# Attention and a mixture of experts on one core: an output's addition moved behind a search's comparisons, and the last expert's routing moved forward

## The chip, the cores and the metric

The kernel runs on one core of one Trainium2 chip. The metric is the device time of one execution in microseconds (us). Three executions of the kernel before took 903.22, 905.01 and 906.87 us, so the median is 905.01 us. One further execution was profiled; it took 904.79 us, of which the profile's span, from the first to the last instruction, is 903.0 us.

## What is computed

First an attention over 8 batches, 12 heads, 448 positions and a head size of 64, with scores squeezed by a tanh; then a mixture of 8 experts over the 3584 rows of 768 numbers that come out of it.

```
scores = cap * tanh((scale * q @ k.T) / cap)
attn   = exp(scores - max) / sum
x      = (attn @ v) as N x D                  # 3584 x 768
logits = x @ w_gate                           # 3584 x 8
order  = argsort(-logits.flatten())
for idx in order:                             # greedy, best pair first
    tok, e = idx // E, idx % E
    if assigned[tok] >= 0 or counts[e] >= cap: continue
    assigned[tok] = e; counts[e] += 1         # cap = 3584 / 8 = 448
for e in range(E):
    h = relu(x[assigned == e] @ w1[e])        # 448 x 1024
    out[assigned == e] = h @ w2[e]            # 448 x 768
```

The greedy assignment is sequential in the reference. The kernel does it expert by expert: it finds which expert fills up first, fixes that expert's 448 rows, takes them out, and goes on. So the experts come out in an order that the data sets, one every round, and each one's rows are known only when its search is done.

## The kernel before

The first 330 us or so are the attention and the gate's logits. From then on TensorE (PE) computes one expert after the other. The text calls the p-th expert in the order of routing "turn p", with p from 0 to 7.

**The two GEMMs of a turn.** A turn has 320 large matmuls, and a counter `now` counts them; `rt.place` is this counter modulo 320, "the place". `ffn1` has 8 units `f` of 18 matmuls (L855, 128 x 448), 144 in all: 6 chunks of the 768 inputs, times three products, because each fp32 operand is split in a high and a low part (`xgh`, `xgl` and `w1h`, `w1l`). `ffn2` has 8 units `u` (L883, 128 x 384): the token blocks 0 to 3 for the left half of the outputs (`hf` 0, `u` 0 to 3), then the same for the right half. Blocks 0 to 2 have 24 matmuls, block 3 (64 tokens) has 16. Its result is in two halves of 64 rows, so ScalarE (ACT) copies the lower one to `y` (L892) and VectorE (DVE) adds it to the upper one, which is still in PSUM (L893). The result tiles `psH` are three, in rotation; a unit's slot is free again when its last reader is done.

**The search beside it.** The routing of turn p+1 is computed while PE works on turn p. It is a generator (`phases0`): each `yield n` says after how many further matmuls the next piece is to be issued, a negative number gives an absolute place. A piece's instructions are put into the engines' queues in just that order, and each engine runs its own queue strictly in order. `select` is one search by thresholds, in rounds: DVE compares all values with 3 or 7 thresholds (L504, `cmpD`; ACT takes two of seven in later rounds, `cmpA`, L501), PE adds the counts up (L508), DVE picks the next thresholds (L512, L516). There are three searches for an expert, A, B and C; A has 4 rounds with 3, 7, 7 and 3 comparisons, and in its first two rounds DVE does all of them. A runs beside the second GEMM of a turn; B begins at its end, and its first L508 stands three matmuls into the next turn. `finalise` makes the list of rows out of the search's result: a few small DVE operations (L605 to L611), two matmuls (L617, L618), more DVE operations (L621 to L635), four matmuls (L639), and so on to `idx` (L651). The table `LK` holds the place at which `finalise` is issued, for each turn.

**The DMA turn of x.** As soon as a turn's rows are known, GpSimd (POOL) gathers them (`gather`, L790). PE needs x with the inputs on the partitions. From turn 3 on (`FT=3`) DMAs do that: four `planes` on ACT split the 32-bit numbers in 16-bit halves (L812, `pl`) and store them (L813, `xz`), and two transposed loads on the queue of SyncE (SP) bring them back (L816): the first after two planes, the second after four. `cutt` then makes `xgh` on ACT (L822) and `xgl` on DVE (L823), in unit `u` 6. The planes are issued 26, 34, 42 and 50 matmuls after the gather; they stand in the list `xq`, which `tick` looks through after each matmul: the entry at its head is run when the counter has reached its number.

**Weights.** SP loads `w1r` and `w2r` in pieces, four and three buffers of them; ACT makes the high part and POOL the low part of each (`cut`, L758 and L762, `w1l` and `w2l`). POOL also issues the scatter of finished outputs (L868).

The lines that the change touches are the table `LK` (L327), the `yield` in `finalise` (L614) and the addition in `ffn2` (L893).

Of the kernel before, what the change touches and what calls it, by code (L numbers as in the profile page):

```python
# [323 lines left out]


YL=[]
LK=(0,0,145,132,132,132,132,128); FT=3  # L327
ACF=1
LF=1
TA=0  # L330
# [2 lines left out]
class Routing:  # L333
# [267 lines left out]
    def finalise(s,wp,L,update):  # L601
        nc=s.nc; T=s.T; NC=s.NC; v=nc.vector
# [8 lines left out]
        v.tensor_scalar(ei,s.e8s[0:1],-1.0,8.0,op0=ALU.mult,op1=ALU.add)  # L611
        s.ei=ei
        if s.cur>=FT: s.early(s.cur,ei)
        yield 8 if s.cur==1 else 18 if s.cur>=FT else 12  # L614
        ps=s.psum()
        warm=(lambda n: s.warm(n)) if s.cur==0 else (lambda n: None)
        nc.tensor.matmul(ps[:112,0:2],s.lo,sc[:,:,NC-1],start=True,stop=False)  # L617
# [19 lines left out]
        ps=s.psum()  # L637
# [8 lines left out]
        ps=s.psum()  # L646
# [25 lines left out]
    def phases0(s,wp,L,turned):  # L672
        HA=[7,10]; HB=3
        for p in range(s.E):
# [5 lines left out]
            yield from (s.search(wp,turned if p==0 else ()) if p<s.E-1 else s.last(wp))  # L680
            yield -((p-1)*320+LK[p]) if p>1 else 4
            yield from s.finalise(wp,L,p<s.E-1)
# [3 lines left out]
def ffn_all(nc, tc, ctx, rt, xs, xz, w1, w2, out, ident, E, wp, deferred, xctx, gen):  # L686
# [44 lines left out]
    def need(p):  # L731
        while len(res)<=p: step()
# [67 lines left out]
    def xtr(p,c):  # L800
        if p>=E or c is None: return
        newx(p)
        gather(p)
        ps=pt.tile([128,512],F32,name="psX")
        for j,(o,n) in enumerate(TS):
            nc.tensor.transpose(ps[:,o:o+128],row(j)[:,c*128:c*128+128],ident)
        cutx(p,c,ps)
# [22 lines left out]
    def tick(n=1):  # L830
        cnt[0]+=n; bc[0]+=n; now[0]+=n
        if bc[0]>=BG:
            if pend: bc[0]=0; scatter(*pend.pop(0))
        if len(res)>cur[0]+1 and cur[0]+1 not in xgs:
            bc[0]=0; n=cur[0]+1; gather(n)
            if n>=FT:
                xq.extend((now[0]+TD+TJ*j,lambda j=j: planes(j)) for j in range(4))
        while xq and xq[0][0]<=now[0]: xq.pop(0)[1]()
        if cnt[0]>=hint[0]:
            cnt[0]=0; step()  # L840
# [23 lines left out]
    ons={}; scat=[]  # L864
# [9 lines left out]
    def ffn2(p,t,hf,cs,work={}):  # L874
        if p not in ons: ons[p]=(f2.tile([128,3*DM],F32,name="on"),f2.tile([64,DM],F32,name="on3"))
        ps=ph.tile([128,512],F32,name="psH")
        h=hh[p]
        o,n=TS[t]
        terms=((o,0),(512+o,0),(o,1)) if t<3 else ((o,0),(o,1))
        m=0; nm=FC*len(terms)  # L880
        for f in range(FC):
            for a,w in terms:
                nc.tensor.matmul(ps[:,:HD],h[:,f,a:a+128],spl[p,2,hf,f//2][w][:,f%2,:],start=(m==0),stop=(m==nm-1))  # L883
                m+=1
                tick()
                if m%8==4 and m//8<len(cs): xtr(p+1,cs[m//8])
                for z in work.get(m,()): z()
        cols=slice(hf*HD,hf*HD+HD)
        if t<3: nc.scalar.activation(ons[p][0][:,t*DM+hf*HD:t*DM+hf*HD+HD],ps[:,:HD],AF.Copy)  # L889
        else:  # L890
            y=f2.tile([64,HD],F32,name="y3",bufs=2)
            nc.scalar.activation(y,ps[64:128,:HD],AF.Copy)  # L892
            nc.vector.tensor_tensor(ons[p][1][:,cols],ps[:64,:HD],y,op=ALU.add)  # L893
    need(0)
    WG=3; NW=23; WJ=4
    for i in range(WG): load1(0,i)
# [13 lines left out]
    for p in range(E):  # L910
# [12 lines left out]
        if lastp:  # L923
            while pend: scatter(*pend.pop(0))
            ih=f2.tile([128,2],I32,name="ih")
            for k in range(2): nc.gpsimd.tensor_scalar(ih[:,k:k+1],res[p][0][:,2:3],2.0,float(k),op0=ALU.mult,op1=ALU.add)
            nc.gpsimd.drain()
            lp[0]=False
            out2=out.rearrange("n (q d) -> (n q) d",q=2)
            for t,hf in [(t,hf) for t in (3,0,1,2) for hf in range(2)]:  # L930
                ffn2(p,t,hf,[])
                if t==2: put(out2,ih[:,hf:hf+1],ons[p][0][:,t*DM+hf*HD:t*DM+hf*HD+HD])
                elif hf==1: scatter(p,t)
            break
        for u in range(8):
            if p+1<FT:
                if u==4: load1(p+1,0); load1(p+1,1)
                if u==5: load1(p+1,2); load2(p+1,0)
            if u==6:
                if p+1>=FT: load1(p+1,2); load2(p+1,0)  # L940
                load1(p+1,3)
            if u==7: load2(p+1,1)
            wk=({5:{14:[lambda: split1(p+1,0)]},6:{8:[lambda: split1(p+1,1)]}} if p+1<FT else {5:{2:[lambda: split1(p+1,0)],12:[lambda: split1(p+1,1)]}}).get(u,{})
            if p<1 and u==7: wk={15:[lambda: xtr(1,3)]}
            if p+1>=FT and not lastp:
                for m,k,c in {6:[(5,0,0),(9,1,0),(12,0,3),(15,1,3)]}.get(u,()): wk[m]=wk.get(m,[])+[lambda k=k,c=c: cutt(p+1,k,c,c+3)]
            ffn2(p,u%4,u//4,(CL if p<1 else CP)[u] if p+1<FT else [],wk)
            if u>3: pend.append((p,u%4))
# [59 lines left out]
```

## Time and profile before

| | |
|---|---|
| median of three executions | 905.01 us |
| profiled execution | 904.79 us |
| its span | 903.0 us |
| first L855 of turns 2 to 7 | 514.30, 581.58, 649.02, 714.74, 776.41, 838.28 us |
| granted TensorE clock over the span | 0.994 |

A row of a timeline gives the start in us, the duration, the engine, the line in the code, the operation, the tile written and the tiles read with their shapes, and in brackets how long the engine had stood idle before and what ended that. A row of waits gives the total, the number of times and the longest. Neighbouring matmuls overlap in the rows (0.34 us each, one every 0.17 us), so a wait is read from the starts.

### The profile page before, as it was taken

The numbers are of one execution on the slowest core, as the hardware profiler recorded it, in microseconds if no ns is written. First come the engines' busy times: TensorE is split into PE (matmuls) and PEld (weight loads), VectorE is DVE, ScalarE is ACT, GpSimd is POOL, SyncE is SP. The second block draws the span as 40 slices with busy tenths as digits, with TensorE's granted clock in tenths as the row PEclk, the third lists the DMA queues.
The fourth block names the chain that finished last, engine by engine and source line by source line (L and its number), as shares of the span: only waits on it lengthen the run. The fifth ranks groups of instructions, "written<-read, shape, count | busy, mean of one in ns | idle before, by whom it ended". The sixth has DMA issues, their size and how long they took to land.

```text
span 903.0 us, 17418 instructions
## 1 busy us (share of the span) xinstructions
PE 867.1 (96%) x6222; PEld 635.0 (70%) x6222; DVE 608.5 (67%) x2012; ACT 585.2 (65%) x836; POOL 350.6 (39%) x506
## 2 busy tenths in 40 slices
PE   7999999999999997899999999899899899999997
PEld 3333444444333345789989989889889889989997
DVE  3788888989888888766776776776776775240210
ACT  6998898989899948273582673573573664434521
POOL 7100000000000009482593492492492592774751
PEclk9999999999999999999999999999999999999999
DMA  8799999996994017751825525925925926927801
GB/s 120 116 133 136 133 172 171 140 171 118 201 170 70 1 61 244 246 160 52 277 75 171 163 71 158 293 75 157 287 82 166 296 63 179 310 71 202 287 10 53
DMA packets 321463, 136.84 MB, mean 152 GB/s; under 512 B 252288, under 2 KB 303232, under 8 KB 320864
## 3 DMA queue, kind: packets, MB, share of 16 engines
q1 hardware_dynamic: 312304, 106.59, 53.9%
q0 software_dynamic: 4656, 22.02, 7.2%
q10 hardware_dynamic: 4416, 7.11, 2.4%
q8 instruction: 49, 0.80, 0.4%
q14 instruction: 38, 0.31, 0.1%
HBM read 97.15 MB, written 31.65 MB: 143 GB/s over the span
## 4 chain that ended last, share of the span: by engine, by line
PE 76%; DVE 6%; issue 5%; DMA 5%; ACT 3%; SPq 3%; POOL 2%; ACTq 0%; POOLq 0%; DVEq 0%
PE psH L855 23%; PE psH L883 19%; PE psA L189 12%; PE psS L148 11%; PE psM L206 4%; DMA xg<-xs,idx 2%; PE psS L153 2%; DVE cmpD L504 2%; SPq L92 2%; ACT pl L812 1%; PE psM L37 1%; DMA w1r<-in_moe_w_dram 1%; DVE es L165 1%; DMA k<-in_k_dram 1%; PE psL L37 1%
## 5 line engine op out<-in xcount | busy, mean ns | idle before, releaser
L883 PE MATMUL psH<-w2h,hh 128*128 128x384 f32 x896 | 244.9, 343 | 0.0
L883 PE MATMUL psH<-w2l,hh 128*128 128x384 f32 x512 | 175.5, 343 | 0.0
L154 ACT ACTIVATE e<-psS 128x896 f32<-128x896 f32 x168 | 147.5, 909 | 30.5 <-PE psS L148 17.8
L883 PEld LDWEIGHTS psH<-w2h,hh 128*128 128x128 f32 x896 | 164.1, 191 | 0.2
L159 ACT ACTIVATE e<-e,bias 128x1792 f32<-128x1792 f32 (+2 forms) x74 | 147.2, 1991 | 2.0
L855 PE MATMUL psH<-xgh,w1h 128*128 128x448 f32 x384 | 143.4, 374 | 0.3 <-ACT xgh L827 0.3
L855 PE MATMUL psH<-xgh,w1l 128*128 128x448 f32 x384 | 141.5, 368 | 0.0
L855 PE MATMUL psH<-xgl,w1h 128*128 128x448 f32 x384 | 141.0, 367 | 0.0
L148 PE MATMUL psS<-tq,tk 64*64 64x448 f32 x1152 | 131.0, 549 | 6.1 <-ACT e L154 3.9
L762 POOL TENSOR_TENSOR w1l<-w1r,w1h 128x768 fp32r<-128x768 f32 x62 | 114.6, 1851 | 18.3 <-ACT w1h L758 13.0
L189 PE MATMUL psA<-e,nv 64*64 64x448 f32 x1104 | 120.3, 539 | 1.0 <-DVE xT L199 1.0
L762 POOL TENSOR_TENSOR w2l<-w2r,w2h 128x768 fp32r<-128x768 f32 x64 | 118.3, 1849 | 6.2 <-ACT w2h L758 6.0
L460 POOL TENSOR_SCALAR r_Bt<-r_b 112x4 f16<-112x4 int32 x1 | 0.2, 201 | 303.7 <-DVE rin L243 303.7
L165 DVE TENSOR_TENSOR es<-es,e 64x896 f32<-64x896 f32 (+2 forms) x74 | 100.3, 1356 | 2.6 <-ACT e L159 1.3
L883 PEld LDWEIGHTS psH<-w2l,hh 128*128 128x128 f32 x512 | 97.4, 190 | 0.0
L148 PEld LDWEIGHTS psS<-tq,tk 64*64 64x64 f32 x1152 | 43.6, 133 | 72.7 <-issue 38.0
L889 ACT ACTIVATE on<-psH 128x384 f32<-128x384 f32 x48 | 23.5, 490 | 104.1 <-PE psH L883 102.4
L863 DVE SCALAR_TENSOR_TENSOR hh<-psH,hh 128x64 fp32r<-128x64 f32 (+1 forms) x128 | 44.0, 385 | 65.3 <-ACT hh L861 63.4
L189 PEld LDWEIGHTS psA<-e,nv 64*64 64x64 f32 x1104 | 46.0, 133 | 59.5 <-issue 50.5
L868 POOL DMA_INDIRECT out_dram<-on,idx x31 | 32.5, 1047 | 123.1 <-ACT on L889 94.3
L855 PEld LDWEIGHTS psH<-xgh,w1h 128*128 128x128 f32 x384 | 72.6, 189 | 5.5 <-ACT xgh L827 0.5
L855 PEld LDWEIGHTS psH<-xgh,w1l 128*128 128x128 f32 x384 | 72.3, 188 | 5.6 <-POOL gap L760 0.2
(337 smaller groups left out, 1320.8 us busy)
## 6 DMA issues: line engine op xcount, KB each, us to landing
w1r<-in_moe_w_dram SPq DMA_DIRECT2D x64, 384.0 KB, 5.3
w2r<-in_moe_w_dram SPq DMA_DIRECT2D x32, 768.0 KB, 7.4
k<-in_k_dram SPq DMA_DIRECT2D x92, 112.0 KB, 3.4
q<-in_q_dram SPq DMA_DIRECT2D x92, 112.0 KB, 4.0
nv<-in_v_dram SPq DMA_DIRECT2D x72, 128.0 KB, 3.8
xz<-pl ACTq DMA_DIRECT2D x15, 384.0 KB, 3.2
xs<-xn SPq DMA_DIRECT2D x4, 1344.0 KB, 7.2
xs<-xn SPq DMA_DIRECT2D x4, 896.0 KB, 5.1
```

The source lines that it names most:

```text
L148: for c in range(2): nc.tensor.matmul(ps[c*64:c*64+64,h,:S],tks[g,0][hp,o,u*128+c*64:u*128+c*64+64],tks[g,1][hp,o,:],start=True,stop=True)
L154: nc.scalar.activation(ev(g,r),ps[:,:,:S],AF.Tanh,scale=sr[0])
L159: act=lambda: nc.scalar.activation(e,e,AF.Exp,scale=sr[1],bias=bias)
L165: t=es_t[g]; add=lambda o,a,b: nc.vector.tensor_tensor(o,a,b,op=ALU.add)
L189: nc.tensor.matmul(avp[g,o][h*64:h*64+64,:S],lhs,rhs[hp,h,:],start=(j==0 and x==0),stop=j==3)
L206: nc.tensor.matmul(ps[g*32:g*32+32,:S],lhs,rhs,start=first,stop=last)
L762: (eng or nc.gpsimd).tensor_tensor(view(l),r,view(h).bitcast(F32),op=ALU.subtract)
L855: nc.tensor.matmul(ps[:,:C],a[:,c,:],b[:,c,:],start=(m==0),stop=(m==DC*3-1)); m+=1
L863: nc.vector.scalar_tensor_tensor(h[:,d:d+b-a],ps[:,a:b],0.0,h[:,a:b].bitcast(F32),op0=ALU.max,op1=ALU.subtract)
L868: st=nc.gpsimd.indirect_dma_start(out=dst,out_offset=bass.IndirectOffsetOnAxis(ap=ix,axis=0),in_=src,in_offset=None)
L883: nc.tensor.matmul(ps[:,:HD],h[:,f,a:a+128],spl[p,2,hf,f//2][w][:,f%2,:],start=(m==0),stop=(m==nm-1))
L889: if t<3: nc.scalar.activation(ons[p][0][:,t*DM+hf*HD:t*DM+hf*HD+HD],ps[:,:HD],AF.Copy)
```

## The change

Three lines are changed.

```diff
-LK=(0,0,145,132,132,132,132,128); FT=3
+LK=(0,0,145,132,132,132,132,100); FT=3
...
         if s.cur>=FT: s.early(s.cur,ei)
-        yield 8 if s.cur==1 else 18 if s.cur>=FT else 12
+        yield 8 if s.cur==1 else 30 if s.cur==7 else 18 if s.cur>=FT else 12
...
             y=f2.tile([64,HD],F32,name="y3",bufs=2)
             nc.scalar.activation(y,ps[64:128,:HD],AF.Copy)
-            nc.vector.tensor_tensor(ons[p][1][:,cols],ps[:64,:HD],y,op=ALU.add)
+            add=lambda: nc.vector.tensor_tensor(ons[p][1][:,cols],ps[:64,:HD],y,op=ALU.add)
+            if hf==0 and FT-1<=p<E-1: xq.append((now[0]+20,add))
+            else: add()
```

The addition of `u` 3 (`hf` 0, place 232) is put into `xq` for 20 matmuls later, in turns 2 to 6. On DVE, in turn 2, beside search A's first and second round:

```order
 L512 SCALAR_TENSOR_TENSOR fl,th<-psR,r_H8A 128x4
 L516 TENSOR_SCALAR r_H8A,nt<-r_C8A,th 128x7
-L893 TENSOR_TENSOR on_6498<-psH,y_6697 64x384
 L504 TENSOR_SCALAR cmpD,r_ce_309<-r_VAt,th 128x224
 L504 TENSOR_SCALAR cmpD,r_ce_309<-r_VAt,r_H8A 128x224 x6
 L512 SCALAR_TENSOR_TENSOR fl,th<-psR,r_H8A 128x8
 L516 TENSOR_SCALAR r_H8A,nt<-r_C8A,th 128x7
+L893 TENSOR_TENSOR on_6498<-psH,y_6697 64x384
 L504 TENSOR_SCALAR cmpD,r_ce_310<-r_VAt,th 128x224
 L504 TENSOR_SCALAR cmpD,r_ce_310<-r_VAt,r_H8A 128x224 x4
```

The addition stood ahead of the second round's seven comparisons; now it stands behind them and behind that round's result, ahead of the third round's five. Turns 3 and 4 read the same. In turns 5 and 6 DVE's order beside the addition is unchanged.

In turn 6, where the eighth expert's rows are made (there is no search left: the last expert takes what remains), `finalise` is issued 28 matmuls earlier and its first `yield` is 12 longer. On DVE, where `hh` is the reader of a unit of the first GEMM (L863, two instructions a unit), it now reads, from the fifth unit's `hh` on:

```order
L863 SCALAR_TENSOR_TENSOR hh<-psH,hh 128x384
L605 TENSOR_SCALAR gt<-qq,wB 112x32
L606 TENSOR_SCALAR gteq<-qq,wB 112x32
L607 SCALAR_TENSOR_TENSOR gteq<-r_kk,e8s,gt 112x32
L609 SCALAR_TENSOR_TENSOR scan<-r_ones_173,gteq 112x64
L611 TENSOR_SCALAR ei<-e8s 1x1
L863 SCALAR_TENSOR_TENSOR hh<-psH,hh 128x64
L863 SCALAR_TENSOR_TENSOR hh<-psH,hh 128x384
L863 SCALAR_TENSOR_TENSOR hh<-psH,hh 128x64
L863 SCALAR_TENSOR_TENSOR hh<-psH,hh 128x384
L621 SCALAR_TENSOR_TENSOR pG<-scan,psR,gteq 112x32
```

Before, L605 to L611 came two units later, behind the seventh `hh`, and one pair of `hh` stood between L611 and L621. On PE, before, L617 stood two matmuls into the second GEMM (L883):

```order
L855 MATMUL psH<-xgh,w1l 128x448
L883 MATMUL psH<-w2h,hh 128x384 x2
L617 LDWEIGHTS r_lo
L617 MATMUL psR<-scan,r_lo 112x2
L618 LDWEIGHTS r_up
L618 MATMUL psR<-scan,r_up 112x1
```

Now it stands 14 matmuls ahead of the first GEMM's end, and in the place where it was, two matmuls further on, stands L639:

```order
L855 MATMUL psH<-xgh,w1l 128x448
L883 MATMUL psH<-w2h,hh 128x384 x2
L883 MATMUL psH<-w2l,hh 128x384
L883 MATMUL psH<-w2h,hh 128x384
L639 LDWEIGHTS oi
L639 MATMUL psR<-oj,oi 128x224
```

What follows from the rows' list comes about 16 matmuls earlier with it: the gathers on POOL, the planes on ACT (the first two now stand ahead of the copy of `u` 1's result, L889), the transposed loads on SP. The value load of the expert's number and the first two `w1r` loads on SP are issued right behind L611, as before.

## The prediction

> **What bounds the kernel now.** I read the page's chain of work first, then PE's waits from 480 us to the end, then the busy time by expert. "Turn p" is the p-th expert in the order of routing (0 to 7); "place n" is the n-th of the 320 large matmuls of a turn. The chain, by engine:
>
> ```profile
> PE 76%; DVE 6%; issue 5%; DMA 5%; ACT 3%; SPq 3%; POOL 2%; ACTq 0%; POOLq 0%; DVEq 0%
> ```
>
> PE holds 76% of the chain, so a change is worth what PE waits less. PE's waits of the expert part (us in total, times, longest):
>
> ```profile
> PE psR L508 <- DVE cmpD L504: 9.1, 3, 3.1
> PE psR L617 <- DVE ei L611: 1.3, 1, 1.3
> ```
>
> There are only four, one in each of turns 2, 3, 4 and 6. The windows from each turn's first L855 to the next one's, turns 2 to 6 (length, then the engines' busy time, clock, DMA share and rate):
>
> ```profile
> 514.30:581.58 67.28, 64.18 (x348) 59.41 (x348) 47.90 (x221) 37.32 (x71) 38.09 (x42) 0.97 0.50 149
> 581.58:649.02 67.44, 64.34 (x348) 59.42 (x348) 46.99 (x230) 38.46 (x74) 38.12 (x42) 0.97 0.57 171
> 649.02:714.74 65.72, 62.78 (x349) 57.86 (x349) 47.27 (x230) 38.35 (x74) 38.66 (x42) 1.00 0.59 175
> 714.74:776.41 61.67, 61.67 (x338) 57.70 (x338) 35.63 (x171) 34.93 (x63) 37.61 (x40) 1.00 0.59 171
> 776.41:838.28 61.87, 60.61 (x329) 57.94 (x329) 17.57 (x41) 29.22 (x42) 38.28 (x42) 1.00 0.63 190
> ```
>
> Turn 5, where no search runs beside the second GEMM, has no wait. In turns 2 and 3 the granted clock is 0.97. What stands behind the three long waits shows in turn 2, on DVE, ACT and PE:
>
> ```profile
> 564.35 0.55 DVE L893 TENSOR_TENSOR on<-psH,y 64x384 f32<-64x384 f32 x1 [3.04 <-ACT y L892]
> 564.82 0.43 DVE L504 TENSOR_SCALAR_CACHE_REDUCE cmpD<-r_VAt,th 128x224 bf16<-128x224 f16 x1
> ...
> 567.39 0.08 DVE L504 DVE_READ_ACCUMULATOR cmpD<-r_VAt,r_H8A 128x1 bf16 x1
> ```
> ```profile
> 563.83 0.49 ACT L892 ACTIVATE y<-psH 64x384 f32<-64x384 f32 x1 [0.62 <-ACT pl L812]
> ```
> ```profile
> 564.08 0.34 PE L883 MATMUL psH<-w2l,hh 128*128 128x384 f32 x1
> 567.52 0.19 PE L508 MATMUL psR<-r_ce,r_bo 128*128 128x8 bf16 x1 [3.10 <-DVE cmpD L504]
> ...
> 571.93 0.18 PE L508 MATMUL psR<-r_ce,r_bo 128*128 128x8 bf16 x1
> ...
> 582.00 0.18 PE L508 MATMUL psR<-r_ce,r_bo 128*128 128x8 bf16 x1
> ...
> 634.89 0.18 PE L508 MATMUL psR<-r_ce,r_bo 128*128 128x8 bf16 x1 [3.10 <-DVE cmpD L504]
> ...
> 639.36 0.18 PE L508 MATMUL psR<-r_ce,r_bo 128*128 128x8 bf16 x1
> ...
> 649.45 0.18 PE L508 MATMUL psR<-r_ce,r_bo 128*128 128x8 bf16 x1
> ...
> 702.18 0.18 PE L508 MATMUL psR<-r_ce,r_bo 128*128 128x8 bf16 x1 [2.94 <-DVE cmpD L504]
> ...
> 705.09 0.18 PE L508 MATMUL psR<-r_ce,r_bo 128*128 128x8 bf16 x1
> ...
> 715.16 0.18 PE L508 MATMUL psR<-r_ce,r_bo 128*128 128x8 bf16 x1
> ```
>
> DVE stands at the addition L893 for 3.04 us, because ACT reaches `y` only behind the copies of `planes` (pl L812). Seven comparisons are queued behind the addition, and PE's L508 needs all seven.
>
> **The additions of turns 2 to 4.** Without the addition in front, the comparisons begin at 564.35 - 3.04 = 561.31 and take 567.39 + 0.08 - 564.82 = 2.65 us: done at 563.96. L508 stands two matmuls behind the one at 564.08, at about 564.4, so its wait goes. That is 3.10 + 3.10 + 2.94 = 9.1 us. More goes with it. From this L508 to the next, with the same sixteen matmuls between, PE took 4.41 us in turn 2 and 4.47 in turn 3, but 2.91 in turn 4. The clock of 0.97 in those two windows says the same: after a wait of 3.1 us the matmuls ran slow for a while, after 2.94 they did not. 1.50 + 1.56 = 3.1 us. **Gain: 12.2 us.**
>
> By the Trainium skill ("TensorE: Matmul & The Clock Gate", What's actually happening) the clock halves after an idle window of about 3.4 us. By that the 3.10 us waits would not have cooled anything and the 3.1 us would stay; the rows, with slow matmuls only behind these two waits, speak against it.
>
> In its new place the addition stands ahead of the third round's five DVE comparisons. `y` is long there, so it costs its step, 564.82 - 564.35 = 0.47 us. In turn 4, where the clock is whole, that round ended as follows, 0.41 us ahead of its L508 at 705.09:
>
> ```profile
> 704.59 0.09 DVE L504 DVE_READ_ACCUMULATOR cmpD<-r_VAt,r_H8A 128x1 bf16 x1
> ```
>
> So it is short by about 0.1 us a turn: **+0.3**. In turns 5 and 6 nothing of a search stands behind the addition, which there has the wait for the transposed x as cover: nothing.
>
> **What is late next.** PE now runs 4.6 us earlier in turns 2 and 3 and 2.94 in turn 4, but x's second transposed load does not: its issue follows gather, planes and the first load, all ahead of the removed wait. Issue and landing time in turns 2, 3, 4:
>
> ```profile
> L816 SPq DMA_TRANSPOSE xg<-xz x1: 2505/2505/2505, 568.1 to 568.1; - x1
> DMA to landing us min/median/max: 4.6/4.6/4.6
> ...
> L816 SPq DMA_TRANSPOSE xg<-xz x1: 2852/2852/2852, 636.9 to 636.9; - x1
> DMA to landing us min/median/max: 6.1/6.1/6.1
> ...
> L816 SPq DMA_TRANSPOSE xg<-xz x1: 2332/2332/2332, 703.0 to 703.0; - x1
> DMA to landing us min/median/max: 4.5/4.5/4.5
> ```
>
> In turn 5, where PE already runs without a wait, ACT did wait for this load, and the last `xgl` came 775.40 + 2.36 - 774.68 = 3.1 us behind its landing:
>
> ```profile
> 774.68 1.99 ACT L822 ACTIVATE xgh<-xg 128x576 fp32r<-128x576 f32 x3 [3.79 <-DMA xg<-xz]
> 775.40 2.36 DVE L823 TENSOR_TENSOR xgl<-xg,xgh 128x576 fp32r<-128x576 f32 x3 [3.48 <-ACT xgh L822]
> ```
>
> In turns 2 to 4 the first comparisons of search B are queued behind `xgl` on DVE: five of them, 1.9 us (five sevenths of 2.65), and PE's L508 three matmuls into the next turn (582.00, 649.45, 715.16) needs them. Ready is issue + landing + 5.0. With the mean landing of 5.1 us: 578.2, 647.0, 713.1. Due without the old waits: 577.4, 644.8, 712.2. **New wait: 0.8 + 2.2 + 0.9 = 3.9 us.** All at 4.5 us would give 2.1; all at 6.1 gives 1.8 + 3.2 + 1.9 = 6.9, with 1.5 more if the 3.2 cools the clock. I take the mean, because the landing depends on what else is on the queues and the scatter moves ahead of this load.
>
> **The eighth expert's routing, in turn 6.** L605 to L611 stand 28 matmuls earlier, L617 at place 130 instead of 146, L639 at 148 instead of 164. Before (DVE, POOL, PE):
>
> ```profile
> 802.73 0.69 DVE L863 SCALAR_TENSOR_TENSOR hh<-psH,hh 128x64 fp32r<-128x64 f32 x2 [2.96 <-ACT hh L861]
> 803.34 1.68 DVE L605 TENSOR_SCALAR gt<-qq,wB 112x32 f32<-112x32 f32 x1
> 804.93 1.90 DVE L606 TENSOR_SCALAR gteq<-qq,wB 112x32 f16<-112x32 f32 x1
> ...
> 808.31 0.19 DVE L624 SCALAR_TENSOR_TENSOR pi<-pG,pE 112x32 int16<-112x32 f32 x1
> ...
> 809.74 0.42 DVE L635 TENSOR_TENSOR oi<-oh,r_idc 112x512 f16<-112x512 f16 x1
> ```
> ```profile
> 803.14 1.84 POOL L762 TENSOR_TENSOR w2l<-w2r,w2h 128x768 fp32r<-128x768 f32 x1
> ...
> 804.98 1.82 POOL L762 TENSOR_TENSOR w2l<-w2r,w2h 128x768 fp32r<-128x768 f32 x1
> ```
> ```profile
> 805.60 0.51 PE L883 MATMUL psH<-w2h,hh 128*128 128x384 f32 x2
> 807.37 0.16 PE L617 MATMUL psR<-scan,r_lo 112*112 112x2 f16 x1 [1.26 <-DVE ei L611]
> ```
>
> L605 and L606 each ended when a split of POOL ended: one such DVE operation passes per split, and L617 waited for that, 1.26 us. Earlier, L605 to L607 lie beside splits too, but have 30 matmuls of 0.20 us ((805.60 - 776.41) / 144 of the first GEMM) until L617 in place of 18, more than three splits (5.5 us); that wait goes. Then L621 cannot start before the second `hh` pair is done at 803.42, and the last two splits still run to 806.8. If they hold the eight operations from L621 to L635 alike, the first ends near 805.0, the second at 806.8, and the other six take 809.74 + 0.42 - 808.31 = 1.85: 808.7. L639 stands four matmuls behind 805.60, near 806.3. It would wait 2.4 us. **Net +1.0**; without that hold -1.3 (the chain, 2.3 us from 803.4, is in time); at worst, with the scan and L611 held too, +1.4. I take +1.0, by the two rows that were held. The two w1 loads, the value load on SP and the four gathers come earlier with it; SP's next work behind them is the transposed load, which waits for planes that come later, so nothing queues behind them; PE has no wait in turn 7 that they could remove.
>
> **Sum.** 904.8 (the profiled execution: span 903.0 and 1.8 around it) - 12.2 + 0.3 + 3.9 + 1.0 = 897.8. It lay 0.2 below the median of 905.01, so I say **898.0**.
>
> **Rivals.**
> *No new wait.* The load lands in time and POOL holds nothing: 904.8 - 12.2 + 0.3 - 1.3 = 891.6; with the hold in turn 6 alone 893.9. For it: turn 5 runs at 61.67 us with the same load. Against it: turn 5 has no comparisons behind `xgl`. 0.22.
> *The load takes it back.* All landings at 6.1 us, clock cooled once: 897.8 + 3.0 + 1.5 = 902.3. For it: turn 3's landing. 0.12.
> *The slow matmuls stay*, as the page on the clock gate would have it: 897.8 + 3.1 = 900.9. 0.04.
> *The change does not do it*: another input of the comparisons is late too, 904 to 906. The threshold is there at 561.31 by the rows. 0.03.
> *Slower.* The addition reads `psH`, of which there are three, so unit 6's first matmul waits for it. In turn 2 the addition ends near 565.9 (L508 at 564.4, then the round's threshold, then 0.5), and unit 6 starts 43 matmuls of 0.18 us (2.91 / 16) ahead of the L508 due at 577.4, near 569.7. It decides only if the addition is over 3.8 us late, and gives more than 909.5 only with (909.5 - 898.0) / 3 = 3.8 us of wait beyond that, in each of three turns. 0.02.
>
> **How the numbers follow.** A measurement tells about 0.5% (4.5 us) from no change. The forecast, 895 to 900.3, has 0.57. The range, 893.0 to 902.4, leaves out half of the first rival, the last two and half of the tail. Faster by over 0.5% (below 900.5): forecast and first rival, 0.79. Within it: second, third and fourth, 0.19. Slower: 0.02.
>
> **What would show it.** Right: no wait at the second L508 of search A and a clock of 1.00 in turns 2 and 3; windows of turns 2 to 6 near 62.8, 63.7, 65.1, 62.6 and 62.9 us (a wait at search B falls into the next turn's window); ACT waiting for xg<-xz in turns 2 to 4, and PE's new waits at the first L508 of search B and, in turn 6, at L639 instead of L617. Wrong: turns 3 and 4 at 62.8 too, with no such waits (first rival), or L508 still late behind L893. A landing far from 5 us would move the forecast most.

## The result, and the profile after

| | median | runs | ratio to before |
|---|---|---|---|
| before | 905.17 us | 903.22 to 906.87 (4) | |
| after | 897.49 us | 894.71 to 898.33 (4) | 0.991 (0.9881 to 0.994) |

The change makes the kernel 0.9% faster. The profiled execution took 898.33 us (span 896.6), against 904.79 (span 903.0). One execution of the run "routing only", further down, took 4890.56 us; it counts in that run's median and not in its ratio.

PE's waits from 480 us to the end, after (us in total, times, longest):

```profile
PE psR L508 <- DVE cmpD L504: 4.1, 3, 3.0
PE psR L639 <- DVE oi L635: 1.6, 1, 1.6
PE psR L617 <- DVE ei L611: 0.2, 1, 0.2
```

The line that named search A's comparisons before names L508 again, three times, but 4.1 us in place of 9.1. It is another L508, as the timelines show. The windows of turns 2 to 6, each from its first L855 to the next turn's (length, busy time of the engines, clock, DMA share and rate):

```profile
514.84:577.47 62.63, 62.63 (x347) 57.92 (x347) 44.16 (x207) 34.80 (x65) 37.59 (x40) 1.00 0.47 134
577.47:643.69 66.22, 63.15 (x349) 57.88 (x349) 49.93 (x238) 40.74 (x81) 40.15 (x43) 1.00 0.59 179
643.69:707.14 63.45, 62.89 (x349) 57.87 (x348) 47.16 (x231) 38.47 (x74) 38.90 (x43) 1.00 0.61 186
707.14:769.57 62.43, 61.88 (x339) 57.70 (x338) 36.40 (x178) 34.60 (x63) 37.78 (x42) 1.00 0.63 184
769.57:832.13 62.56, 60.78 (x328) 57.86 (x328) 23.43 (x42) 29.52 (x43) 39.59 (x44) 1.00 0.69 207
```

Their sum went from 323.98 to 317.29 us: turn 2 became 4.65 us shorter, turns 3 and 4 1.22 and 2.27 us shorter, turns 5 and 6 0.76 and 0.69 us longer. A wait at the start of a turn lies in that turn's window, though the search belongs to the turn before. The clock is 1.00 in all five.

Turn 2 on DVE, after. First the comparisons of A's second round, the addition behind that round, then `xgl` and search B:

```profile
561.77 0.44 DVE L504 TENSOR_SCALAR_CACHE_REDUCE cmpD<-r_VAt,th 128x224 bf16<-128x224 f16 x1
...
564.34 0.09 DVE L504 DVE_READ_ACCUMULATOR cmpD<-r_VAt,r_H8A 128x1 bf16 x1
...
565.38 0.55 DVE L893 TENSOR_TENSOR on<-psH,y 64x384 f32<-64x384 f32 x1
...
577.12 2.37 DVE L823 TENSOR_TENSOR xgl<-xg,xgh 128x576 fp32r<-128x576 f32 x3 [4.01 <-ACT xgh L822]
...
581.24 0.09 DVE L504 DVE_READ_ACCUMULATOR cmpD<-r_qt,r_T8B 128x1 bf16 x1
```

On ACT and PE in the same turn:

```profile
576.40 1.99 ACT L822 ACTIVATE xgh<-xg 128x576 fp32r<-128x576 f32 x3 [4.45 <-DMA xg<-xz]
```
```profile
564.80 0.18 PE L508 MATMUL psR<-r_ce,r_bo 128*128 128x8 bf16 x1
...
581.38 0.18 PE L508 MATMUL psR<-r_ce,r_bo 128*128 128x8 bf16 x1 [2.97 <-DVE cmpD L504]
```

The second round is done at 564.43, its L508 runs at 564.80 without a wait, and the addition no longer waits for `y`. Then ACT stands 4.45 us for the second transposed load, DVE behind ACT, search B's comparisons behind `xgl`, and PE behind these: 2.97 us. In turns 3 and 4 the same place waits 0.56 and 0.55 us (ACT and PE):

```profile
639.85 1.99 ACT L822 ACTIVATE xgh<-xg 128x576 fp32r<-128x576 f32 x3 [1.69 <-DMA xg<-xz]
...
703.30 2.00 ACT L822 ACTIVATE xgh<-xg 128x576 fp32r<-128x576 f32 x3 [1.68 <-DMA xg<-xz]
```
```profile
644.83 0.18 PE L508 MATMUL psR<-r_ce,r_bo 128*128 128x8 bf16 x1 [0.56 <-DVE cmpD L504]
...
708.27 0.18 PE L508 MATMUL psR<-r_ce,r_bo 128*128 128x8 bf16 x1 [0.55 <-DVE cmpD L504]
```

Turn 6 on DVE, POOL and PE, after:

```profile
792.37 1.93 DVE L607 SCALAR_TENSOR_TENSOR gteq<-r_kk,e8s,gt 112x32 f16<-112x32 f16 x1
794.33 1.90 DVE L609 TENSOR_TENSOR_SCAN scan<-r_ones,gteq 112x64 f16<-112x64 f16 x1
...
797.40 0.56 DVE L621 SCALAR_TENSOR_TENSOR pG<-scan,psR,gteq 112x32 f32<-112x32 f16 x1
797.88 1.91 DVE L622 SCALAR_TENSOR_TENSOR pE<-scan,psR,gteq 112x32 f32<-112x32 f16 x1
...
801.26 0.42 DVE L635 TENSOR_TENSOR oi<-oh,r_idc 112x512 f16<-112x512 f16 x1
```
```profile
796.09 1.82 POOL L762 TENSOR_TENSOR w2l<-w2r,w2h 128x768 fp32r<-128x768 f32 x1
...
797.91 1.83 POOL L762 TENSOR_TENSOR w2l<-w2r,w2h 128x768 fp32r<-128x768 f32 x1
```
```profile
796.29 0.16 PE L617 MATMUL psR<-scan,r_lo 112*112 112x2 f16 x1 [0.20 <-DVE ei L611]
...
801.74 0.56 PE L639 MATMUL psR<-oj,oi 112*128 112x224 f16 x4 [1.58 <-DVE oi L635]
```

L607, the scan and L622 each took 1.9 us, as long as one of POOL's splits (the subtractions that make `w1l` and `w2l`). The scan took 0.29 us in the profile before, where POOL's last split had ended at 806.80:

```profile
807.03 0.29 DVE L609 TENSOR_TENSOR_SCAN scan<-r_ones,gteq 112x64 f16<-112x64 f16 x1
```

L639 waited 1.58 us for the operations behind L622.

### The profile page after: what moved, and what is told of

It is laid out like the page before. It is cut to its first block, busy times and chain, and to the rows that moved or that the text cites. A ratio compares the mean times of both kernels' runs of the same rounds, so it can differ in the third digit from the quotient of the medians.

```text
span 896.6 us, 17418 instructions
## 1 busy us (share of the span) xinstructions
PE 862.6 (96%) x6222; PEld 631.5 (70%) x6222; DVE 613.7 (68%) x2012; ACT 584.8 (65%) x836; POOL 352.7 (39%) x506
## 4 chain that ended last, share of the span: by engine, by line
PE 69%; issue 12%; POOL 5%; DVE 5%; DMA 4%; SPq 2%; ACT 2%; POOLq 0%; ACTq 0%; DVEq 0%
PE psH L855 20%; PE psH L883 15%; PE psA L189 12%; PE psS L148 10%; PE psM L206 4%; DMA xg<-xz 2%; PE psS L153 2%; SPq L92 2%; POOL w1l L762 2%; POOL out_dram L868 1%; DVE cmpD L504 1%; PE psM L37 1%; DVE es L165 1%; POOL xg L790 1%; DMA k<-in_k_dram 1%
## 5 line engine op out<-in xcount | busy, mean ns | idle before, releaser
L883 PE MATMUL psH<-w2h,hh 128*128 128x384 f32 x896 | 243.0, 340 | 0.0
L883 PE MATMUL psH<-w2l,hh 128*128 128x384 f32 x512 | 174.2, 340 | 0.0
L883 PEld LDWEIGHTS psH<-w2h,hh 128*128 128x128 f32 x896 | 162.1, 188 | 0.2
L855 PE MATMUL psH<-xgh,w1h 128*128 128x448 f32 x384 | 143.4, 373 | 0.3 <-ACT xgh L827 0.3
L855 PE MATMUL psH<-xgh,w1l 128*128 128x448 f32 x384 | 141.3, 368 | 0.0
L855 PE MATMUL psH<-xgl,w1h 128*128 128x448 f32 x384 | 141.0, 368 | 0.1
L883 PEld LDWEIGHTS psH<-w2l,hh 128*128 128x128 f32 x512 | 96.4, 188 | 0.0
L889 ACT ACTIVATE on<-psH 128x384 f32<-128x384 f32 x48 | 23.4, 488 | 100.3 <-PE psH L883 93.8
L863 DVE SCALAR_TENSOR_TENSOR hh<-psH,hh 128x64 fp32r<-128x64 f32 (+1 forms) x128 | 43.9, 384 | 58.6 <-ACT hh L861 56.7
L868 POOL DMA_INDIRECT out_dram<-on,idx x31 | 34.4, 1110 | 117.8 <-ACT on L889 87.7
L861 ACT ACTIVATE hh<-psH 128x448 fp32r<-128x448 f32 x64 | 34.8, 543 | 65.6 <-PE psH L855 54.9
L855 PEld LDWEIGHTS psH<-xgh,w1h 128*128 128x128 f32 x384 | 72.6, 189 | 5.5 <-ACT xgh L827 0.5
```

The lines of the kernel that those rows point to most:

```text
L855: nc.tensor.matmul(ps[:,:C],a[:,c,:],b[:,c,:],start=(m==0),stop=(m==DC*3-1)); m+=1
L861: nc.scalar.activation(h[:,:C],ps[:,:C],AF.Relu)
L863: nc.vector.scalar_tensor_tensor(h[:,d:d+b-a],ps[:,a:b],0.0,h[:,a:b].bitcast(F32),op0=ALU.max,op1=ALU.subtract)
L868: st=nc.gpsimd.indirect_dma_start(out=dst,out_offset=bass.IndirectOffsetOnAxis(ap=ix,axis=0),in_=src,in_offset=None)
```

## The experiments

All times are medians; the ratio is to runs of the kernel before on the same chip (905 to 906 us).

| run | us | ratio, 95% interval |
|---|---|---|
| addition only | 897.78 | 0.9899 (0.9876 to 0.9923) |
| routing only | 906.69 | 1.0004 (0.9986 to 1.0021) |
| without the second load | 892.21 | 0.9839 (0.9815 to 0.9862) |
| search B first | 894.72 | 0.9866 (0.9842 to 0.9889) |
| L639 later | 894.81 | 0.9882 (0.9863 to 0.99) |
| both moves | 893.06 | 0.9861 (0.9839 to 0.9882) |
| busy wait | 901.32 | 0.9959 (0.9943 to 0.9975) |

**The two parts of the change, each alone.** Against the changed kernel:

```diff
-LK=(0,0,145,132,132,132,132,100); FT=3
+LK=(0,0,145,132,132,132,132,128); FT=3
-        yield 8 if s.cur==1 else 30 if s.cur==7 else 18 if s.cur>=FT else 12
+        yield 8 if s.cur==1 else 18 if s.cur>=FT else 12
```

> The change without its second part: the addition is moved, the eighth expert's routing stays at place 128 with 18 matmuls to its first matmul. Theory (the addition gives all the gain, the second part costs about 0.5 us): PE's waits at the second L508 of search A gone, the waits at search B's first L508 as with the whole change (3 to 5 us in sum), in turn 6 again 1.3 us at L617 and none at L639; time 0 to 1.5 us below the whole change, about 897. Rival (the second part helps too): 1 us or more above the whole change.

And the reverse, against the kernel before:

```diff
-LK=(0,0,145,132,132,132,132,128); FT=3
+LK=(0,0,145,132,132,132,132,100); FT=3
-        yield 8 if s.cur==1 else 18 if s.cur>=FT else 12
+        yield 8 if s.cur==1 else 30 if s.cur==7 else 18 if s.cur>=FT else 12
```

> The change's second part alone: the addition stays where it was. Theory: the three waits of 2.9 to 3.1 us at the second L508 of search A stay, with the slow matmuls behind them; turn 6 waits about 1.6 us at L639 instead of 1.3 at L617; time within 1.5 us of before, 905 to 906.5. Rival (the second part helps by itself): 903 or less.

The addition alone gives the whole change's time, and the routing alone gives before's, within the intervals. PE's waits with the addition only:

```profile
PE psR L508 <- DVE cmpD L504: 3.7, 3, 2.5
PE psR L617 <- DVE ei L611: 1.3, 1, 1.3
```

With the routing only:

```profile
PE psR L508 <- DVE cmpD L504: 9.1, 3, 3.1
PE psR L639 <- DVE oi L635: 1.6, 1, 1.6
PE psR L617 <- DVE ei L611: 0.5, 1, 0.5
```

So the second part takes away a wait of 1.3 us and brings waits of 1.8 to 2.1: turn 6 lasts 61.87 us without it, as before, and 62.56 (whole change) or 62.86 us (routing only) with it. By the medians its cost is too small to tell.

**Without the second transposed load.** The last 192 rows of each expert from turn 3 on are taken as they were gathered, so these rows of the output are not the reference's.

```diff
-        if r:
+        if r and k==0:
             n=o+n-2*128*k
```

> The whole change, without the second transposed load of x in turns 2 to 6: the last 192 rows of an expert are taken as they were gathered, so the outputs of these rows are wrong. Theory (search B's comparisons wait behind xgl, and that for this load): PE's waits at search B's first L508, 4.1 us in three turns, are gone or under 0.3 us each; time about 4 us below the whole change, 893 to 894. Rival (they wait for DVE's or ACT's own work, or for the first load): they stay at 2 us or more in sum.

The only wait of PE that is left in the expert part, and the windows of turns 2 to 6:

```profile
PE psR L617 <- DVE ei L611: 0.6, 1, 0.6
```
```profile
514.83:577.45 62.62, 62.62 (x347) 57.95 (x347) 48.02 (x221) 37.18 (x71) 38.65 (x42) 1.00 0.50 153
577.45:640.18 62.73, 62.73 (x349) 57.91 (x349) 47.13 (x230) 38.36 (x74) 38.67 (x42) 1.00 0.56 177
640.18:702.91 62.73, 62.73 (x349) 57.91 (x348) 47.11 (x230) 38.36 (x74) 38.64 (x42) 1.00 0.58 181
702.91:764.58 61.67, 61.67 (x338) 57.73 (x338) 36.79 (x172) 35.58 (x64) 38.66 (x42) 1.00 0.55 174
764.58:826.08 61.50, 60.77 (x328) 57.95 (x328) 20.66 (x39) 28.45 (x40) 38.02 (x42) 1.00 0.65 205
```

All waits at search B went with the load, so the load was what they came from. The weight loads behind it on SP start earlier in this run as well (the first at 566.18 us instead of 571.60 in turn 2); the next run, which keeps the load where it is, leaves these out. The gain, 5.3 us by the medians and 6.1 by the profiled executions, is more than the expected 4. By the windows 5.0 us of it come from search B, more than the 4.1 that are listed as waits, and 1.1 from turn 6, which lost its wait at L639: POOL's last split ends there at 793.52, just as L622 begins, and L622 took 0.24 us. The four runs lie between 892.08 and 892.35 us.

**Search B ahead of the load.** The load stays; the first comparisons of search B are issued 19 matmuls earlier, and their L508 stays at its place.

```diff
-        if s.cur>FT: yield max(0,306-s.place()-4)
+        if s.cur>FT: yield max(0,287-s.place()-4)
...
-            s.pos='A'; yield max(6,12-s.since()) if s.cur==1 and s.since()<20 else 16 if m==7 and s.place()>304 else max(13,18-s.since()) if m==7 and s.since()<20 else s.hA+1*(s.cur==1)+(3 if m==7 else 0)+(3 if alone and i else 0); s.pos=''
+            s.pos='A'; yield max(6,12-s.since()) if s.cur==1 and s.since()<20 else 35 if s.cur>FT and ab=="B" and i==0 else 16 if m==7 and s.place()>304 else max(13,18-s.since()) if m==7 and s.since()<20 else s.hA+1*(s.cur==1)+(3 if m==7 else 0)+(3 if alone and i else 0); s.pos=''
```

> The whole change, and in turns 2 to 4 search B's first comparisons are issued between the first and the second part of xgl, so on DVE and ACT they stand ahead of the work that waits for the second load; PE's order is the same. Theory: the waits at search B's first L508 go (4.1 us), xgl ends as before since DVE was idle meanwhile, and at most 0.3 us a turn come back at the next turn's first matmuls; time 893 to 894.5. Rival (PE needs the second load itself by then): the same wait turns up at an L855 that reads xgl, and the time stays at 897.

It took 894.72 us, just above the expected range. PE's waits:

```profile
PE psR L639 <- DVE oi L635: 1.6, 1, 1.6
PE psR L508 <- DVE cmpD L504: 1.4, 2, 1.0
PE psR L617 <- DVE ei L611: 0.4, 1, 0.4
```

The waits at search B's first L508 are gone, and none came at an L855: in this run PE did not need the second load itself by then, only the comparisons that stood behind it. But 1.4 us came back at another L508, that of search C. Turn 3 there, on ACT, DVE and PE:

```profile
652.86 0.84 ACT L758 ACTIVATE w1h<-w1r 128x768 fp32r<-128x768 f32 x1 [2.48 <-DMA w1r<-in_moe_w_dram]
```
```profile
654.91 0.69 DVE L863 SCALAR_TENSOR_TENSOR hh<-psH,hh 128x64 fp32r<-128x64 f32 x2 [2.36 <-ACT hh L861]
655.51 0.44 DVE L553 SCALAR_TENSOR_TENSOR r_qt<-r_qt,th,psV 128x224 f16<-128x224 f16 x1
```
```profile
656.87 0.18 PE L508 MATMUL psR<-r_cd,r_bo 128*128 128x4 bf16 x1 [1.00 <-DVE cmpD L504]
```

The chain is of the same kind as at the additions: ACT waits for a DMA, here a piece of weights, ACT's copy of a unit's result and with it DVE's `hh` stand behind that, and search C behind `hh`. That PE has come nearer to the weights, now that the earlier waits are gone, is the likely reason; it was not tried.

**L639 later in turn 6.** Against the changed kernel, ahead of L639:

```diff
-        yield 18
+        yield 30 if s.cur==7 else 18
```

> The whole change, with 30 instead of 18 matmuls between L617 and L639 of the eighth expert's routing (L639 at place 160). Theory (L639 waits because POOL's last two splits hold DVE's operations from L621 on): its wait of 1.6 us goes, none comes at L647, the row list comes 2 us later and PE does not feel it; time 1.5 us below the whole change, 896, if the clock falls alike. Rival (the later row list makes the transposed x late for turn 7): the gain is lost to a wait at turn 7's first L855.

Turn 6, from 768.96 to 829.43 us, has no wait of PE any more:

```profile
768.96:829.43 60.47, 60.47 (x329) 57.95 (x328) 22.51 (x41) 28.97 (x42) 38.88 (x43) 1.00 0.68 201
```

It is 2.1 us shorter than in the changed kernel, by the waits at L639 and L617 (1.6 and 0.2 as listed, 1.75 and 0.4 read from the starts). The later row list did not cost anything at turn 7's start. The whole run is 2.7 us faster than the changed kernel, where 1.5 were expected; 1.0 us of that lies in turn 3's window, ahead of anything that the edit touches: turn 2's load took 7.0 us from issue to ACT's start there, and 7.5 in the changed kernel. So the earlier L617 pays only with this second step.

**Both moves.** The edits of the last two in one kernel.

> Search B's first comparisons ahead of the second part of xgl, and L639 later, in one kernel. Theory: no wait at search B's first L508 and none at L639; what is left is the wait of 0.4 to 1.4 us at search C's first L508, where weights come late, and 0.2 to 0.6 at L617; time 892.5 to 893.5. Rival (the two share their gain): 894 or more.

893.06 us, the fastest complete kernel here, 1.4% below before. PE's waits in the expert part:

```profile
PE psR L508 <- DVE cmpD L504: 0.7, 1, 0.7
PE psR L617 <- DVE ei L611: 0.2, 1, 0.2
```

**A busy wait.** The kernel before, with PE kept at work while it waits; the results of these matmuls are not used.

```diff
             ps=s.psum()
+            if s.cur>FT and ab=="A" and i==1: s.warm(8,ps)
             nc.tensor.matmul(ps[:,:m+1],s.bo,cd,start=True,stop=True)
```

> The kernel before, with eight matmuls of 128 x 128 whose result is not used ahead of each second L508 of search A in turns 2 to 4, so that PE works for about 1 us of the 3 us that it stands there. They change nothing of when L508 can run. Theory (a wait of this length lets the clock fall in some turns and not in others, which costs about 1.5 us each time, and it is the standstill that does it): no slow matmuls behind these waits, clock 1.00 in turns 2 to 4, time 901 to 902.5 and runs that lie closer together than before's 6 us. Rival (the slow matmuls have another cause): clock and time as before, 905 to 906.

Turn 2 on PE (L508 is line 509 in this kernel; the eight matmuls are sixteen rows in the profile, and take 1.95 us, not about 1), and stretches that roughly cover turns 2, 3 and 4, with the clock in the third column from the right:

```profile
564.62 1.95 PE L714 MATMUL psR<-ident 128*128 128x128 f32 x16
567.94 0.17 PE L509 MATMUL psR<-r_ce,r_bo 128*128 128x8 bf16 x1 [1.38 <-DVE cmpD L504]
```
```profile
515.00:582.00 67.00, 65.62 (x370) 60.75 (x369) 48.60 (x223) 38.25 (x72) 38.68 (x42) 1.00 0.50 152
582.00:648.00 66.00, 64.40 (x364) 59.62 (x363) 47.15 (x230) 38.27 (x74) 38.68 (x42) 1.00 0.58 177
648.00:712.00 64.00, 62.57 (x354) 58.06 (x353) 46.09 (x226) 37.20 (x73) 38.69 (x42) 1.00 0.58 175
```

PE still stands at L508 for the comparisons behind `y`, but the longest standstill is 1.6 us in place of 3.1, the clock stays at 1.00, and the kernel is 3.5 us faster than before. Its six runs lie within 1.7 us of each other (900.78 to 902.46), before's eleven beside them within 5.1 (902.96 to 908.01).

## Why the prediction came out as it did

The time, 897.5 us, lies 0.5 us from the forecast of 898.0, and the waits went and came where the prediction put them. Their sizes were off, in both directions, so it is partly luck that the sum came so near. The sizes can be read from the windows: the run without the second load has the moved addition and no wait in turns 2 to 5, so its windows (62.62, 62.73, 62.73 and 61.67 us) show what these turns take without waits.

| term, us | forecast | by the windows |
|---|---|---|
| turns 2 to 4: waits, slow matmuls, moved addition | -11.9 | -12.4 |
| new waits at search B | +3.9 | +5.0 |
| eighth expert's routing | +1.0 | +0.7 |
| sum of turns 2 to 6 | -7.0 | -6.7 |

A listed wait is counted from the end of the matmul before it, and that matmul is 0.34 to 0.37 us long where the next would start 0.17 to 0.21 us after its start. So each wait costs nearly 0.2 us more than is listed.

- **The three waits behind the addition** are gone, as the order on DVE said. Addition only and routing only show that the whole gain comes from there. The prediction took their listed 9.1 us, which is about 0.5 too little. L508 stands directly behind the matmul at 564.08, not two further on, so it was due a little earlier than the prediction says; the comparisons were in time all the same.
- **The slow matmuls behind them** are gone too: 1.00 in turns 2 and 3. The busy wait, which shortens only the standstill, agrees with the forecast 3.1 us: 3.5 by the medians, 2.7 by the profiled executions. The reading that the length decides (3.1 us cools, 2.94 does not) was wrong. With the addition only, the clock fell after 2.53 us; with the routing only, after 2.92; in the changed kernel it did not after 2.97.
- **The addition in its new place** was put at 0.3 us. From the second to the third L508 of search A PE now takes 3.02 us in each of the three turns, instead of the 2.91 of turn 4 before: 0.3.
- **The new wait at search B** was put at 0.8 + 2.2 + 0.9 = 3.9 us. It is listed as 2.97 + 0.56 + 0.55 = 4.1 and cost 3.5 + 0.7 + 0.8 = 5.0 by the windows. The mechanism is shown by the two runs without the load and with the comparisons ahead of it, and the 5.0 us from the landing to L508 were right in all three turns (576.40 to 581.38, 639.85 to 644.83, 703.30 to 708.27). The split was wrong, and that its sum came near was luck. In turn 2 the landing took 7.5 us (issued 568.9, ACT goes on at 576.40) instead of the mean of 5.1; in turns 3 and 4 it took 4.8 and 5.1, where before had 4.6, 6.1 and 4.5. Turn 3's load was also issued 9.0 us ahead of the moment when PE needs it, not 7.9. Why turn 2's load is the slow one, here and in the runs beside it (2.5 us of wait with the addition only, 2.3 with L639 later), was not tried; with both moves it took 4.6 us. In turn 2 PE needed this load itself as well: the weight load of the first L855 that reads `xgl` waited 0.4 us for L823, and the matmul started 0.47 us after the one before it instead of 0.21. Also, this L508 stands two matmuls into the turn, not three.
- **The eighth expert's routing** was put at +1.0 us (the prediction's own figures, 2.4 less 1.3, give 1.1) and cost 0.7 in the profile. The wait did move from L617 to L639, and by the rows the reason is that POOL's splits hold DVE: the held operations end with a split, and they are short where POOL is idle. Of the eight operations one and a part were held (L622 1.91 us, L621 0.56), not two, and the scan was held as well: 0.20 + 1.58 us of wait, for 2.4 forecast. That one operation passes per split does not hold in general: without the second load L605 alone took 6.82 us from 784.22 on, and ended near 791.0 with the third split that had begun after it.
- **The rivals.** "No new wait" fell with the waits at search B; without the second load its time, 891.6, was nearly reached (892.2). "The load takes it back" came true in turn 2 alone. "The slow matmuls stay" fell with the clock of 1.00, and "the change does not do it" with the L508 at 564.80 that waits for nothing. "Slower" by a slot of `psH`: PE never waited for one.

## What to carry to other kernels

An instruction that waits for another engine's late result also holds all that is queued behind it on its own engine. Moving it behind work that is ready pays; but follow what then arrives first, since an engine that runs earlier meets the next load that does not, and here about 5 of some 12 us were given back there. The same cure worked a second time, on the comparisons that stood behind a DMA. A wait that is only moved forward in the order, like L617's, comes back at the next wait of the same chain unless the chain as a whole has the time.

## What the runs showed of the hardware

**The clock after a standstill.** With the addition only, PE stood 2.53 us in search B. Its rows behind that:

```profile
581.55 0.18 PE L508 MATMUL psR<-r_ce,r_bo 128*128 128x8 bf16 x1 [2.53 <-DVE cmpD L504]
...
582.68 0.36 PE L855 MATMUL psH<-xgl,w1h 128*128 128x448 f32 x1
582.88 0.53 PE L855 MATMUL psH<-xgh,w1l 128*128 128x448 f32 x1
...
586.20 0.43 PE L855 MATMUL psH<-xgh,w1l 128*128 128x448 f32 x1
```

The slow stretch begins 1.3 us after the standstill has ended and lasts 3.3 us, during which a matmul comes every 0.37 us instead of every 0.20. Neither figure is fixed: with the routing only, turn 4's slow stretch began at once behind a standstill of 2.92 us, at 703.51, and lasted 5.8 us, to 709.34.

That a standstill of about the same length cools in one execution, that is, is followed by slow matmuls, and not in another is one source of the scatter of this kernel's times: before's runs beside the experiments have a mean clock of 0.991 to 0.998 and 902.2 to 908.3 us, and the two with 0.998 are the fastest two. It is not the only one, since those with 0.994 alone go from 904.0 to 908.0 us. With the busy wait, where the clock is 0.999 or 1.0, the times lie within 1.7 us; the run without the second load, which has no standstill over 0.7 us from 480 us on, stays within 0.3 us. The Trainium skill ("TensorE: Matmul & The Clock Gate", What's actually happening) says that the window of the activity monitor, which sets the clock, runs freely, which agrees with both outcomes at one length; its figure of about 3.4 us of idleness does not, as 2.5 us were enough here.

**A scan held by POOL.** The scan L609 took 1.90 us beside a split and 0.29 without one. That agrees with the Trainium skill ("SBUF — State Buffer", Who interferes with whom), by which a DVE instruction with two SBUF inputs contends with a GpSimd instruction that reads SBUF. The two `hh` pairs between them, which read PSUM, were not held: 1.26 us for four instructions, beside the split that began at 796.09. No run took the splits away by themselves.
